# The mean of the first tile by an add-and-accumulate over two half rows, in place of a sum over 512 elements, with the first turns reordered

## The chip, the cores and the metric

One core of a Trainium2 chip. The metric is the device time of one execution in microseconds (us); several executions were taken of each kernel and their median is quoted. A ratio is the mean time of one kernel's runs over that of the other's runs of the same rounds, so it is not quite the ratio of the medians that stand beside it. Faster or slower needs 2%. Where the text calls a kernel slower, it means only that its 95% interval lies clear of 1.

## The reference, cut to what matters

```python
x = A_x                                  # (1, 2048, 512) bf16: 16 tiles of 128 rows
xn = _layernorm(x, axis=-1)
return x + _A_ref(xn, ...) + _B_ref(xn, B_w_gate, B_w_up, B_w_down)
# _B_ref: (gelu(xn @ w_gate) * (xn @ w_up)) @ w_down, 512 -> 1376 -> 512
```

The first matrix work that can start is `xn @ w_gate` and `xn @ w_up` for the first tiles. The kernel does not wait for the whole normalisation there: it multiplies the *centred* rows, x minus mean, and brings in the division by the standard deviation when it reads the result.

## The kernel before

The parts that the change touches. `V`, `ACT` and `PE` record an operation on VectorE (DVE), ScalarE (ACT) and TensorE (PE) with an estimated duration. A list scheduler orders what was recorded: PE and the queue of loads on SyncE stay in program order, DVE, ACT and GpSimd are ordered by the estimates, and `ch` chains some DVE operations in a fixed order. A filler is a small matmul whose result nobody reads, put in to give PE something to do (0.31 us each in the profile before). A transpose of `cent_T` is a matmul on PE, too (0.22 us at full pace), and ACT then copies its result out (0.28 us for 128 columns), so that PE can use it as weights.

```python
ch(V(lambda e: e.tensor_reduce(SUM0.ap, X[0].ap, mybir.AxisListType.X, ALU.add), 600, [X[0]], [SUM0], "sum0"))
ch(cent(0, 0), cent(0, 1))        # tile 0: D*x - sum, columns 0..127 and 128..511
fill(2)                           # two filler matmuls on PE
cent_T(0, 0, 1, 7)                # PE transpose of the first 128 columns, ACT copies it out (times 1/D)
ch(cent(1, 0), cent(1, 1))        # tile 1: x + (-mean), its mean comes from ACT
fill(1)
ev0 = cent_T(0, 1, 4, 5, True)    # the other three transposes of tile 0
ev1 = cent_T(1, 0, 1, 6)          # the first transpose of tile 1
S.order_behind(ev0(), ev1)        # ACT copies tile 1's first one out ahead of tile 0's other three
ks(0, 0, [0], True)               # k=0, tile 0, gate half: two matmuls of 256 columns
ks(0, 0, [1])                     # the same with the up half
cent_T(1, 1, 4, 7)
ks(0, 1, [0], True)
ks(0, 1, [1])                     # k=0, tile 1
# ... statistics of tile 2 on DVE ...
ks(1, 0, [0])
ks(1, 0, [1])                     # k=1, tile 0: needs the up slice of k=1
cent_T(2, 0, 1, 6)                # transposes of tile 2, and so on
```

The weights of the first 512 columns are loaded in slices of 128 KB, gate and up in turn for k = 0, 1, 2, 3, behind tile 0 of x in one queue. Tiles 1 and 2 of x go through ACT's queue.

## Time and profile before

| | before |
|---|---|
| median of 3 runs before the prediction | 177.34 us (177.23 to 177.38) |
| span in the profile | 175.5 us |
| PE busy | 171.9 us, 98% |
| PE alone, without a hole, from | 6.23 us to 173.56 us |

The span is the time inside the program; the run adds some 1.3 us around it (the profiled run took 176.79 us). PE's busy time is no proof that it is at its best (the warm-up's matmuls of 512 columns follow one another at 0.42 us, later ones at 0.22, and both count as busy), but a chain that is PE alone from 6.23 us to the end says that only what happens before 6.23 us, or a hole made later, can move the time. The lines for this are in the prediction below.

### The profile page before, as it was taken

To read this page: it belongs to the slowest core of one execution; us is meant where nothing else is said; L and a number is where in the kernel's file an instruction comes from. 1 tells how busy PE (TensorE), PEld (TensorE's weight loads), DVE (VectorE), ACT (ScalarE), POOL (GpSimd) and SP (SyncE) were. 2 spreads that over 40 slices of the span, in tenths; PEclk is the share of its full clock that TensorE was granted. 3 is DMA by queue.
4 is the path that set the end of the run, shared out by engine and by line. 5 is a ranking of instruction groups with operands and counts; after the bars stand their busy time and mean duration, and the time that the engine had idled before them with its cause. 6 is when DMAs were issued, how large, how long until landed. Compare 5 with 4: busy or idle time off the path is not lost.

```text
span 175.5 us, 2504 instructions
## 1 busy us (share of the span) xinstructions
PE 171.9 (98%) x876; PEld 84.9 (48%) x891; DVE 160.1 (91%) x278; ACT 95.2 (54%) x187; POOL 10.8 (6%) x24
## 2 busy tenths in 40 slices
PE   8999999999999999999999999999999999999995
PEld 3546464845544444444644444444464444444453
DVE  6987999997989999799999999999999999999931
ACT  5474768999767898465676792000657960000000
POOL 3222030203000000002000000000000000000000
DMA  5999999985998000002033000002001000000311
GB/s 170 242 334 141 268 145 218 114 130 112 195 289 231 4 0 2 0 30 78 15 73 78 0 0 0 4 0 90 30 0 30 4 0 0 0 0 0 120 65 60
DMA packets 32420, 14.36 MB, mean 82 GB/s; under 512 B 23736, under 2 KB 32408, under 8 KB 32408
## 3 DMA queue, kind: packets, MB, share of 16 engines
q1 hardware_dynamic: 32096, 13.94, 34.7%
q10 hardware_dynamic: 312, 0.27, 0.5%
q8 instruction: 7, 0.11, 0.3%
q14 instruction: 5, 0.04, 0.1%
HBM read 6.46 MB, written 2.10 MB: 49 GB/s over the span
## 4 chain that ended last, share of the span: by engine, by line
PE 95%; DMA 2%; SPq 1%; issue 1%; DVE 0%
PE PS L885 37%; PE PS L844 32%; PE PS L750 16%; PE PS L713 4%; PE PS L818 3%; PE PS L702 2%; DMA arena<-in_B_w_up_dram 2%; SPq L484 1%; PE PS L680 0%; SPq L493 0%; DVE arena L903 0%
## 5 line engine op out<-in xcount | busy, mean ns | idle before, releaser
L885 PE MATMUL PS<-arena 128*128 128x512 bf16 (+3 forms) x317 | 65.9, 366 | 0.3
L844 PE MATMUL PS<-arena 128*128 128x512 bf16 x257 | 57.1, 379 | 0.4
L885 PEld LDWEIGHTS PS<-arena 128*128 128x128 bf16 (+1 forms) x323 | 30.8, 98 | 35.2
L844 PEld LDWEIGHTS PS<-arena 128*128 128x128 bf16 x264 | 25.8, 98 | 30.2
L788 DVE TENSOR_TENSOR_SCAN arena<-arena 128x512 bf16<-128x512 f32 x32 | 38.8, 1254 | 0.0
L859 ACT ACTIVATE arena<-PS 128x512 bf16<-128x512 f32 x33 | 19.7, 598 | 25.1 <-DVE arena L903 16.7
L750 PE MATMUL PS<-arena 128*128 128x512 bf16 (+1 forms) x142 | 28.1, 355 | 0.1
L863 ACT ACTIVATE arena<-PS 128x512 bf16<-128x512 f32 x33 | 19.8, 599 | 5.0 <-PE PS L844 4.9
L750 PEld LDWEIGHTS PS<-arena 128*128 128x128 bf16 x144 | 14.1, 98 | 13.3
L877 ACT ACTIVATE PS<-arena 128x512 f32<-128x512 bf16 (+2 forms) x17 | 9.6, 581 | 19.7 <-DVE arena L903 19.0
L759 ACT ACTIVATE arena<-PS 128x512 bf16<-128x512 f32 x32 | 17.5, 596 | 1.5 <-PE PS L750 1.5
L903 DVE TENSOR_TENSOR arena<-PS,arena 128x512 bf16<-128x512 f32 (+2 forms) x17 | 10.8, 652 | 6.3 <-PE PS L885 6.2
L865 DVE TENSOR_TENSOR arena<-arena 128x512 bf16<-128x512 bf16 x33 | 13.2, 420 | 2.6 <-ACT arena L863 2.4
L800 DVE TENSOR_TENSOR arena<-arena 128x4096 bf16<-128x4096 bf16 x4 | 9.2, 2290 | 0.1
L777 DVE TENSOR_TENSOR arena<-arena 128x4096 bf16<-128x4096 bf16 (+1 forms) x5 | 9.2, 1859 | 0.0
L775 DVE TENSOR_TENSOR arena<-arena 128x4096 bf16<-128x4096 bf16 (+1 forms) x5 | 9.2, 1857 | 0.0
L801 DVE TENSOR_TENSOR arena<-arena 128x4096 bf16<-128x4096 bf16 x4 | 9.1, 2286 | 0.0
L611 DVE BATCH_NORM_STATS2 arena<-arena 128x6 f32<-128x512 bf16 x12 | 7.7, 680 | 0.1
L722 ACT ACTIVATE arena<-PS,arena 128x256 bf16<-128x256 f32 (+1 forms) x16 | 6.1, 447 | 2.3 <-DVE arena L557 1.4
L713 PE MATMUL PS<-arena 128*128 128x512 bf16 (+1 forms) x40 | 7.1, 336 | 0.0
L725 DVE SCALAR_TENSOR_TENSOR arena<-PS,arena 128x256 bf16<-128x256 f32 (+1 forms) x16 | 6.3, 445 | 0.7 <-PE PS L702 0.7
L702 PE MATMUL PS<-arena 128*128 128x512 bf16 (+1 forms) x30 | 6.0, 337 | 0.1
(95 smaller groups left out, 124.7 us busy)
## 6 DMA issues: line engine op xcount, KB each, us to landing
out_dram<-arena SPq DMA_DIRECT2D x15, 128.0 KB, 1.7
arena<-in_A_x_dram SPq DMA_DIRECT2D x3, 512.0 KB, 5.5
arena<-in_B_w_down_dram SPq DMA_DIRECT2D x1, 1280.0 KB, 7.2
arena<-in_B_w_gate_dram SPq DMA_DIRECT2D x4, 128.0 KB, 3.1
arena<-in_B_w_up_dram SPq DMA_DIRECT2D x4, 128.0 KB, 3.5
arena<-in_B_w_gate_dram SPq DMA_DIRECT2D x1, 480.0 KB, 6.7
arena<-in_B_w_up_dram SPq DMA_DIRECT2D x1, 480.0 KB, 7.6
arena<-arena SPq DMA_TRANSPOSE x25, 3.1
```

Of the source, the lines that this page charges most:

```text
L702: PE(lambda e: e.matmul(dst, XCd(j, k), WGU[:, ws[0]:ws[-1] + 1, k, f0:f1], start=first, stop=k == KD - 1, skip_group_check=True), d_pe([w ...
L713: ins_ = e.matmul(dst, XCd(j, k), WGU[:, :, k, f0:f1], start=(k == 0), stop=(k == KD - 1))
L750: ins_ = e.matmul(PS[bank][:, 128 * j0:128 * j1], BBT[c][dk].ap[:, 128 * s:128 * (s + 1)], XNT[b].ap[:, dk, 128 * j0:128 * j1], start=(dk ...
L759: GATE["evBu"] = ACT(lambda e, bank=bank, k3=k3, s=s, c=c: e.activation(SSc[k3][s][c].ap, PS[bank][:, :], ACTF.Copy), d_act(512), [BANK[ba ...
L788: V(lambda e, g=g, rb=rb, init=init: e.tensor_tensor_scan(g.ap, rb, g.ap, init, ALU.mult, ALU.add), d_dve_scan(512), [g, PA[RRr]] + ([CARc ...
L844: ins_ = e.matmul(PS[bank][0:m, c0:c1], W.ap[:, dk, 128 * ft:128 * ft + m], XNT[b].ap[:, dk, c0:c1], start=(dk == 0), stop=(dk == KD - 1))
L859: GATE["last_gelu"] = ACT(lambda e, bg=bg, kk=kk, m=m: e.activation(GG[kk].ap[0:m, :], PS[bg][0:m, :], ACTF.Gelu_apprx_tanh), d_act(512), ...
L863: ACT(lambda e, bu=bu, kk=kk, m=m: e.activation(UPB[kk].ap[0:m, :], PS[bu][0:m, :], ACTF.Copy), d_act(512), [BANK[bu]], [UPB[kk]], "evU")
L865: V(lambda e, kk=kk, m=m, ft=ft, k2=k2: e.tensor_tensor(HTt[k2][ft].ap[0:m, :], GG[kk].ap[0:m, :], UPB[kk].ap[0:m, :], ALU.mult), d_dve_tt ...
L877: ACT(lambda e: e.activation(PS[bank][:, c0:c1], X[tt].ap[:, c0:c1], ACTF.Copy), d_act(c1 - c0), [X[tt]], [BANK[bank]], "seed")
L885: ins_ = e.matmul(PS[bank][:, c0:c1], l_[:, 128 * j:128 * (j + 1)], r_[:, c0:c1], start=False, stop=last and n == len(ops) - 1, skip_group ...
L903: V(lambda e: e.tensor_tensor(OUTB[ko].ap[:, c0:c1], PS[bank][:, c0:c1], XD[tt].ap[:, c0:c1], ALU.add), d_dve_1x(c1 - c0), [BANK[bank], XD ...
```

## The change

Its intent is to have the mean of tile 0 sooner: `tensor_reduce` goes over 512 elements (0.69 us in the profile before), while an addition of the two halves of a row with an accumulator output goes over 256 and gives minus the mean at once. Two filler matmuls go, ACT copies the transposes out in the order in which PE makes them, and tile 1's first transpose moves behind the first two matmuls.

```diff
-            if j == 0:
-                f = lambda e: e.tensor_scalar(XN[j].ap[:, c0:c1], X[j].ap[:, c0:c1], float(D), SUM0.ap, ALU.mult, ALU.subtract)
-            else:
-                f = lambda e: e.tensor_scalar(XN[j].ap[:, c0:c1], X[j].ap[:, c0:c1], NM1.ap, None, ALU.add)
+            nm = NM1 if j else NM0
+            f = lambda e: e.tensor_scalar(XN[j].ap[:, c0:c1], X[j].ap[:, c0:c1], nm.ap, None, ALU.add)
 ...
-        ch(V(lambda e: e.tensor_reduce(SUM0.ap, X[0].ap, mybir.AxisListType.X, ALU.add), 600, [X[0]], [SUM0], "sum0"))
+        hd = D // 2
+        ch(V(lambda e: e.tensor_tensor_reduce(H0[2].ap[:, 0:hd], X[0].ap[:, 0:hd], X[0].ap[:, hd:D], scale=-1.0 / D, scalar=0.0,
+                                              op0=ALU.add, op1=ALU.add, accum_out=NM0.ap), 400, [X[0]], [H0[2], NM0], "mean0"))
         ch(cent(0, 0), cent(0, 1))
-        fill(2)
         cent_T(0, 0, 1, 7)
         ch(cent(1, 0), cent(1, 1))
         fill(1)
-        ev0 = cent_T(0, 1, 4, 5, True)
-        ev1 = cent_T(1, 0, 1, 6)
-        S.order_behind(ev0(), ev1)
+        cent_T(0, 1, 4, 5)
 ...
         ks(0, 0, [0], True)
+        cent_T(1, 0, 1, 6)
         ks(0, 0, [1])
```

In `cent_T` the argument `later` and the scale of 1/D for tile 0 are no longer needed.

More of the change, by code (lines that the diff above doesn't have):

```diff
@@ L474, in build @@
         GATE["iotj"] = POOL(lambda e: e.iota(IOTJ.ap, [[1, 512]], base=0, channel_multiplier=0), 600, [], [IOTJ], "iotj")
-        NM1, SUM0 = A.alloc("NM1", [1], F32), A.alloc("SUM0", [1], F32)
+        NM0, NM1 = (A.alloc(n, [1], F32) for n in ("NM0", "NM1"))
         def ld_x(b):
@@ L672, in build, with cent_T @@
         XNp = [[Buf("XN%d_%d" % (j, n), "sb", XN[j].lo + 256 * n, XN[j].lo + (1024 if n else 256)) for n in range(2)] for j in range(2)]
-        def cent_T(j, k0, k1, bank, later=False):
+        def cent_T(j, k0, k1, bank):
             pt = PS[bank].bitcast(BF16)[:, 0:128 * (k1 - k0)]
@@ L684, in cent_T @@
             w = XCs[j] if k1 - k0 == KD else [XCs[j][k0 > 0]]
-            sc = 1.0 if j else 1.0 / D
-            def evac():
-                GATE["evTA"] = ACT(lambda e: e.activation(dst, src, ACTF.Copy, scale=sc), d_act(128 * (k1 - k0)), [BANK[bank]], w, "evT")
-                return GATE["evTA"]
-            return evac if later else evac()
+            GATE["evTA"] = ACT(lambda e: e.activation(dst, src, ACTF.Copy), d_act(128 * (k1 - k0)), [BANK[bank]], w, "evT")
         FR = ((0, 256), (256, 512), (512, 768), (768, 896))
@@ L960, in cent @@
             c0, c1 = (0, 128) if n == 0 else (128, D)
-            if j == 0:
-                f = lambda e: e.tensor_scalar(XN[j].ap[:, c0:c1], X[j].ap[:, c0:c1], float(D), SUM0.ap, ALU.mult, ALU.subtract)
-            else:
-                f = lambda e: e.tensor_scalar(XN[j].ap[:, c0:c1], X[j].ap[:, c0:c1], NM1.ap, None, ALU.add)
-            return V(f, 100 + 0.5 * (c1 - c0), [X[j], NM1 if j else SUM0], [XNp[j][n]], "sub")
-        ch(V(lambda e: e.tensor_reduce(SUM0.ap, X[0].ap, mybir.AxisListType.X, ALU.add), 600, [X[0]], [SUM0], "sum0"))
+            nm = NM1 if j else NM0
+            f = lambda e: e.tensor_scalar(XN[j].ap[:, c0:c1], X[j].ap[:, c0:c1], nm.ap, None, ALU.add)
+            return V(f, 100 + 0.5 * (c1 - c0), [X[j], nm], [XNp[j][n]], "sub")
+        hd = D // 2
+        ch(V(lambda e: e.tensor_tensor_reduce(H0[2].ap[:, 0:hd], X[0].ap[:, 0:hd], X[0].ap[:, hd:D], scale=-1.0 / D, scalar=0.0,
+                                              op0=ALU.add, op1=ALU.add, accum_out=NM0.ap), 400, [X[0]], [H0[2], NM0], "mean0"))
         ch(cent(0, 0), cent(0, 1))
-        fill(2)
         cent_T(0, 0, 1, 7)
```

## The prediction

> **What bounds the kernel now.** I read the page first, for the engines' shares, then the chain that ended last in order of time, then the timeline of the first 7 us engine by engine, and last the DMA issues in narrow stretches, to get the landing of each load.
>
> The page's head and its chain:
>
> ```profile
> PE 171.9 (98%) x876; PEld 84.9 (48%) x891; DVE 160.1 (91%) x278; ACT 95.2 (54%) x187; POOL 10.8 (6%) x24
> ...
> PE 95%; DMA 2%; SPq 1%; issue 1%; DVE 0%
> ```
>
> TensorE (PE) is busy 98% of a span of 175.5 us, and 95% of the chain is PE. A VectorE (DVE) instruction can only shorten this if PE waits for it somewhere. The only DVE piece in the chain (0%) is the last addition of the output. The chain in order of time shows where PE's unbroken run begins:
>
> ```profile
> 2.60 3.59 DMA arena<-in_B_w_up_dram
> 6.19 0.05 issue
> 6.23 0.39 PE PS L702 x2
> 6.62 0.22 PE PS L680 x4
> 6.85 2.81 PE PS L702 x13
> ```
>
> From 6.23 us to 173.56 us the chain holds nothing but PE and gaps of 0.05 us. It is released at 6.23 by a load: the k=1 slice of the up weights, issued at 2.60 and landed 3.59 us later, at 6.19. The start-up before it is a row of small dependent steps, of which the sum of tile 0 is one:
>
> ```profile
> 2.96 0.69 DVE L967 TENSOR_REDUCE arena<-arena 128x1 f32<-128x512 bf16 x1 [0.63 <-DMA arena<-in_A_x_dram]
> 3.68 0.48 DVE L962 TENSOR_SCALAR arena<-arena 128x128 bf16<-128x128 bf16 x2
> 4.13 0.48 DVE L964 TENSOR_SCALAR arena<-arena 128x128 bf16<-128x128 bf16 x2
> 4.76 0.69 DVE L611 BATCH_NORM_STATS2 arena<-arena 128x6 f32<-128x512 bf16 x1
> ...
> 3.83 0.19 ACT L956 ACTIVATION_READ_ACCUMULATOR arena<-arena 128x1 f32 x1
> ...
> 6.23 0.11 PEld L702 LDWEIGHTS PS<-arena 128*128 128x128 bf16 x2 [0.33 <-DMA arena<-in_B_w_up_dram]
> ```
>
> The columns are start, duration, what ran, and in brackets the idle time before it and what ended that. Tile 0 arrives at 2.95, the sum ends at 3.65, the two subtractions of tile 0 run from 3.68, its first transpose on PE starts at 4.00. The last line decides: before the matmul of the up weights, k=1, the weight load (PEld) stood idle 0.33 us for a DMA, though everything from DVE and ScalarE (ACT) was there. So PE already had slack in front of this load.
>
> The landings, from the DMA issues asked for in narrow stretches (issue time plus time to landing, rounded to 0.1): tile 1 of x 0.99 + 2.3 = 3.3; gate k=0 1.20 + 2.4 = 3.6; tile 2 of x about 1.43 + 3.3 = 4.7; up k=0 1.66 + 3.3 = 5.0; gate k=1 2.13 + 3.0 = 5.1; up k=1 2.60 + 3.6 = 6.2.
>
> [...]the accumulator read at 3.83 takes 0.19 us behind an activation of 0.63. [...]the seven warm-up matmuls of 512 columns load weights 0.42 us apart, while 49 later ones take 10.74 us, 0.219 us each. [...]the trace has 2.2 us for the first tile and 3.6 for the up slice.[...]
>
> **The change part by part.** It removes the sum (0.69 us) and adds one add-and-accumulate over two halves of 256. [...]With an accumulator read of 0.06 (the step between dependent DVE rows here is some 0.03 to 0.07) to 0.19 us (ACT's row) it comes to 0.48 to 0.61 us; I take 0.5. The mean is then ready at about 3.46 in place of 3.65, a gain of 0.1 to 0.2 us. The rate could be higher, since a tensor_tensor of 128x512 bf16 takes only 0.42 us in this trace, but the accumulation makes me doubt it.
>
> Tile 0's subtractions use the mean itself in place of D*x minus the sum: same shapes, same 0.48 us for both. They end at about 3.97 rather than 4.16. Tile 1's subtractions wait for ACT's mean, which ends at 3.83 + 0.19 = 4.02, so they move only from 4.13 to about 4.08. The statistics of tile 2 at 4.76 wait for the tile itself (landing about 4.7), and do not move; nor does anything of DVE behind them.
>
> On PE the two filler matmuls before the first transpose go, one stays; the first transpose moves from 4.00 to about 3.8, its evacuation on ACT from 4.32 to about 4.05, and the first real matmul (gate, k=0) from 4.74 to about 4.45. The second pair (up, k=0) needs a load that landed at about 5.0; it starts at 4.96 in the trace, the moment the load is there, and stays. Then the transposes of tile 1, the pair of gate k=0 and the pair of up k=0 for tile 1, and gate k=1 for tile 0 follow in the same set as before, and all this must be done by 6.19, when up k=1 lands. Moved earlier by 0.2 us or not at all, PE waits there. From 6.23 on the program order on PE is that of before. So the sum on the path is **0.0 us**: gain 0.15 to 0.2 at the start, all of it turned into a longer wait for up k=0 and up k=1.
>
> The last part is the order on ACT. Before, the evacuation of tile 1's first transpose (0.28 us) was forced ahead of tile 0's other three (0.49). Now it comes behind. Worked out: tile 0's first 4.05 to 4.33, its other three 4.35 to 4.84, tile 1's first 4.86 to 5.14 (before: 4.87 to 5.15, equal within the guess), tile 1's other three 5.3 to 5.8. PE then has tile 1's four k=0 matmuls from about 5.3 and the gate k=1 pair by 5.7 to 5.9, six matmuls of 0.11 us: in time for 6.19, with 0.3 us to spare. Cost 0.
>
> **The rivals.** (a) The gain goes straight through to the end: 177.34 - 0.2 = 177.15. For it speaks that the sum stands on the path to the first matmul. Against it stand the two landings at 5.0 and 6.2, and the 0.33 us of idle. (b) [...]Against it: the warm-up ends only at 3.92 and the first transpose now follows at 3.8, so there is hardly a hole. (c) The new operation is slower than I think; the trace has no row of it. It may take up to 0.69 + 0.3 = 1.0 us before PE feels it; at 1.5 us it would cost about 0.5, 177.8. (d) The order of later DVE and ACT work is chosen by the kernel's list scheduler from estimated durations; the estimate here falls from 600 to 400 ns and orders far downstream may flip. With PE full, a flip can hardly gain, but could open a hole of some tenths: 177.3 to 178.
>
> **Range and chances.** The centre is the time before, 177.3: cause and slack both say zero. The three runs before lie within 0.15 us of each other. Down I allow 0.4 for an earlier landing of the up slice or part of (a); up I allow 0.6 for (c), (d) and a little of (b). So 176.9 to 177.9. A change of 2% is 3.5 us; nothing named gains that, and only (b) and (d) together approach a loss of it: faster 0.01, same 0.97, slower 0.02.
>
> **What would show each step right or wrong.** In the profile of the changed kernel the new DVE operation starts at about 2.96 and gives way to the subtraction at about 3.46 (right if within 3.35 to 3.6). The first transpose starts near 3.8, the first matmul with gate weights near 4.45, the one with up weights still at about 4.96. The weight load that waits for the up slice is still released at 6.2, with at least as long an idle before it as 0.33, and the chain from there is PE alone for 167.3 us. The statistics of tile 2 stay at 4.76. I am wrong if the release at 6.2 is by ACT or DVE and not by a DMA, if the load lands at another time because loads moved, if PE's rows keep half pace behind 4.3, or if PE shows holes later that were not there.

Rival (b) came to about +1.4 us, 178.8: it was my guess that without the two fillers PE would keep its half pace longer.

"Clock" and "the release of the clock", in the expectations below, are words for what the rows show of PE's pace: in the profile after three transposes take 0.32 us of the chain at half pace (at 4.13) and 0.17 at full pace (at 5.48). The granted clock is 1.0 in every run, and 1.00 in the profile after both from 0.8 to 4.4 us and from 5.2 to 8.0, so what lies behind the two paces is not shown.

## The result, and the profile after

| | before | after |
|---|---|---|
| median | 177.31 us (176.98 to 177.39, 6 runs) | 177.12 us (176.77 to 177.23, 6 runs) |
| ratio | | 0.9987, 95% interval 0.9974 to 1.0000 |
| span in the profile | 175.5 us | 175.5 us |

The medians differ by 0.19 us, which is just what the rival of a gain that passes through had forecast (177.15). So one comparison does not separate "nothing" from "all of it", and the experiments had to.

The head of the page and the chain's shares, after:

```profile
PE 172.7 (98%) x889; PEld 84.9 (48%) x889; DVE 159.6 (91%) x279; ACT 95.9 (55%) x187; POOL 10.7 (6%) x24
...
PE 98%; DVE 0%; issue 0%
```

PE has 889 matmul records here and 876 before, though this program has two fewer of them: some were missing from the trace before, so the 0.8 us more of PE is no finding. What is new is that no load stands in the chain any more. The same chain in order of time (start, duration, what):

```profile
0.77 3.15 PE PS L929 x7
3.92 0.11 PE PS L680
4.03 0.11 PE PS L936
4.13 0.32 PE PS L680 x3
...
4.48 0.59 PE PS L697 x2
5.07 0.11 PE PS L680
5.18 0.30 PE PS L697 x2
5.48 0.17 PE PS L680 x3
5.65 0.95 PE PS L697 x8
6.59 0.22 PE PS L680 x4
```

L929 is the warm-up, L680 the transposes, L697 the matmuls of the first turns. In this execution PE is in the chain from the warm-up on. The transposes of tile 2 (the last line; 6.62 before) come 0.03 us earlier than before, and the matmuls of the second stage start at 10.92 rather than 10.96. So the profiled execution shows a gain of 0.04 us at the end of the first turns, where the mean itself came 0.25 us earlier. Its timeline (start, duration, engine, operation, and in brackets the idle time before it and what ended that):

```profile
2.92 0.43 DVE L961 CUSTOM_DVE_ANT_0 arena<-arena 128x256 bf16<-128x256 bf16 x1 [0.59 <-DMA arena<-in_A_x_dram]
3.27 0.08 DVE L961 DVE_READ_ACCUMULATOR2_ANT arena<- 128x1 f32 x1
3.39 0.48 DVE L957 TENSOR_SCALAR arena<-arena 128x128 bf16<-128x128 bf16 x2
3.70 0.10 PEld L680 LDWEIGHTS PS<-arena 128*128 128x128 bf16 x1 [0.69 <-DVE arena L957]
4.09 0.48 DVE L957 TENSOR_SCALAR arena<-arena 128x128 bf16<-128x128 bf16 x2 [0.22 <-ACT arena L951]
4.48 0.59 PE L697 MATMUL PS<-arena 128*128 128x256 bf16 x2
4.97 0.51 PE L697 MATMUL PS<-arena 128*128 128x256 bf16 x2
5.21 0.28 ACT L685 ACTIVATE arena<-PS 128x128 bf16<-128x128 bf16 x1 [0.23 <-PE PS L680]
5.55 1.05 PE L697 MATMUL PS<-arena 128*128 128x256 bf16 x8
```

The new operation takes 0.43 us and its accumulator read, which overlaps its end, is done at 3.35. The subtractions of tile 0 follow at 3.39, which is 0.47 us after the start of the operation; before it was 0.72. So the mean is 0.25 us sooner. But tile 1's subtractions still wait for ACT, at 4.09 (4.13 before), and the pair with the up half of k=0 starts at 4.97 (4.96 before). The pair of matmuls at 4.48 takes 0.59 us in two overlapping rows; the first two such rows before took 0.38. PE is still at half pace here: a transpose takes 0.31 us and a matmul of 256 columns 0.42, against 0.22 and 0.27 from the three transposes at 5.32 on. Before, the turn came between 4.52 and 4.74 (two rows of PE):

```profile
4.52 0.31 PE L680 MATMUL PS<-arena 128*128 128x128 bf16 x1
4.74 0.27 PE L702 MATMUL PS<-arena 128*128 128x256 bf16 x1
```

This is where the gain went in this execution. The first matmul is 0.26 us earlier (4.48 for 4.74), but the gate pair needs 0.38 us up to the next matmul (4.48 to 4.86) where it needed 0.22 (4.74 to 4.96), and tile 1's transpose, 0.11, now stands before the up pair: 0.38 + 0.11 - 0.22 = 0.27. The up slice of k=0, landed at 1.66 + 3.2 = 4.9, holds nothing up here.

### The profile page after: what moved, and what is told of

Its sections match the earlier page's. It is cut to its first block, busy times and chain, and to the rows that moved or that the text cites. A ratio compares the mean times of both kernels' runs of the same rounds, so it can differ in the third digit from the quotient of the medians.

```text
span 175.5 us, 2521 instructions
## 1 busy us (share of the span) xinstructions
PE 172.7 (98%) x889; PEld 84.9 (48%) x889; DVE 159.6 (91%) x279; ACT 95.9 (55%) x187; POOL 10.7 (6%) x24
## 4 chain that ended last, share of the span: by engine, by line
PE 98%; DVE 0%; issue 0%
PE PS L880 37%; PE PS L839 32%; PE PS L745 16%; PE PS L708 4%; PE PS L697 3%; PE PS L813 3%; PE PS L929 2%; PE PS L680 1%; DVE arena L898 0%; PE PS L936 0%
## 5 line engine op out<-in xcount | busy, mean ns | idle before, releaser
L839 PE MATMUL PS<-arena 128*128 128x512 bf16 x264 | 58.1, 379 | 0.0
L720 DVE SCALAR_TENSOR_TENSOR arena<-PS,arena 128x256 bf16<-128x256 f32 (+1 forms) x16 | 6.3, 443 | 0.4 <-PE PS L697 0.4
L697 PE MATMUL PS<-arena 128*128 128x512 bf16 (+1 forms) x30 | 6.3, 350 | 0.0
```

The costliest lines, as they stand in the source:

```text
L697: PE(lambda e: e.matmul(dst, XCd(j, k), WGU[:, ws[0]:ws[-1] + 1, k, f0:f1], start=first, stop=k == KD - 1, skip_group_check=True), d_pe([w ...
L839: ins_ = e.matmul(PS[bank][0:m, c0:c1], W.ap[:, dk, 128 * ft:128 * ft + m], XNT[b].ap[:, dk, c0:c1], start=(dk == 0), stop=(dk == KD - 1))
```

## The experiments

All twelve runs were in three groups of four; each group ran on one chip with its own runs of before, six executions of each kernel and eleven of before. The differences looked for are a few tenths of a us, and the executions of one kernel in one group spread over 0.5 to 1.1 us, three far ones at 179 us left aside, so I lean on the profiles' rows where the times cannot decide.

One reading serves all of them. Call *start* the moment at which the 40 matmuls of the second stage (6.93 us in the chain, where there is no hole) begin: 10.96 before, 10.92 after. The span minus this start is 164.5 to 164.6 us in the nine profiles (before, after, a_after, b_op_only, c_order_only, d_after_fill, g_load_late, n_after_again, q_none_pinned) where PE has no hole behind it and the turns of the two kernels are kept: 175.5 - 10.96 = 164.5 before, 175.5 - 10.92 = 164.6 after. So the whole difference between such executions arises before 12 us.

### Group one: the parts one by one

**a_after.** The changed kernel, unedited, timed once more.

> The changed kernel itself, once more and timed closely. Load theory (the landing of the up weights of k=1 near 6.0 to 6.2 us sets the start of PE's unbroken run, the earlier mean ends in a longer wait): 177.2 to 177.4, ratio to before within 0.9985 to 1.0005. Pass-through theory (the earlier mean goes to the end): 0.2 us faster, ratio 0.9988 or less with an interval clear of 1. Clock theory[...]: warm pace again only from about 5.2 us in the profile, where before has it from 4.2.

Measured: 177.03 us, before 176.91, ratio 1.0008 (0.9986 to 1.0031). The gain of 0.19 us is not repeated. The chain of this profile:

```profile
1.66 3.60 DMA arena<-in_B_w_up_dram
5.25 0.05 issue
5.30 0.39 PE PS L697 x2
5.69 0.17 PE PS L680 x3
5.86 0.87 PE PS L697 x8
...
11.06 6.93 PE PS L708 x40
```

Here the chain does begin with a load, but with the up slice of k=0 (issued 1.66, landed 5.26), not with that of k=1. And PE is at full pace from the first transpose on (0.23 us at 3.73), with one filler. The clock theory, my guess that with fewer fillers PE turns to full pace some 1 us later, had asked for half pace until 5.2 us. It fails. (That before has full pace from 4.2 is a misreading in the expectation; its transpose at 4.52 is still at half pace, as shown above.)

**b_op_only.** Before, with the new operation alone.

```diff
-ch(V(lambda e: e.tensor_reduce(SUM0.ap, X[0].ap, mybir.AxisListType.X, ALU.add), 600, [X[0]], [SUM0], "sum0"))
+ch(V(lambda e: e.tensor_tensor_reduce(H0[2].ap[:, 0:hd], X[0].ap[:, 0:hd], X[0].ap[:, hd:D], scale=1.0, scalar=0.0,
+                                      op0=ALU.add, op1=ALU.add, accum_out=SUM0.ap), 400, [X[0]], [H0[2], SUM0], "sum0"))
```

> Before with the add-and-accumulate alone (same fillers, same order of turns and evacuations). Mean ready near 3.38 in place of 3.65. Load theory: time of before within 0.1 us, the wait of the weight load for the up slice grows from 0.33 to about 0.4 to 0.6. Pass-through theory: 0.2 us faster. Clock theory: full pace from 4.2 as in before.

Measured: 176.79 us, before 176.91, ratio 0.9989 (0.9970 to 1.0008). It is the lowest median of this group, but the interval holds both nothing and 0.2 us. In this execution the up slices landed early (k=0 at 1.66 + 3.0 = 4.7, k=1 at 2.60 + 3.2 = 5.8), PE waited for neither, so the longer wait that was expected is a miss, and the start was 10.66. PE was at full pace from about 4.4 (0.28 us for the two transposes at 4.35). The first transpose came at 3.93, because the fillers held PE until then: its subtractions had begun at 3.31 already. In c_order_only, without those fillers and with the old sum, it came at 4.04; only both parts of the change together bring it to 3.71.

**c_order_only.** The changed order, with the sum over 512 elements kept (tile 0 as D*x minus the sum, and the scale of 1/D when it is copied out, as before).

```diff
-ch(V(lambda e: e.tensor_tensor_reduce(..., accum_out=NM0.ap), 400, [X[0]], [H0[2], NM0], "mean0"))
+ch(V(lambda e: e.tensor_reduce(SUM0.ap, X[0].ap, mybir.AxisListType.X, ALU.add), 600, [X[0]], [SUM0], "sum0"))
```

> The changed order and fewer fillers, with the sum over 512 elements kept. Load theory: time of before within 0.1 us. If the gain of the changed kernel is one of the order, it is here too (0.1 to 0.2 us faster). Clock theory: as in the changed kernel the pace is half until about 5.2 us, and with the mean 0.27 us later the first turns end 0.1 to 0.3 us later than before: 177.4 to 177.6.

Measured: 177.19 us (one execution at 179.15), ratio 1.0028 (0.9986 to 1.0069). In the profile PE's weight loads wait for both up slices, 0.27 us for k=0 at 5.28 and 0.33 us for k=1 (landed 6.5) at 6.54, the start is 11.27, and the pace turns at about 4.8 us with one filler (0.31 us for the transpose at 4.46, 0.27 for the matmul at 4.91). The chain of this profile runs through the sum (3.01, 0.69 us) and has only 0.05 us of waiting before each of the two matmuls: here the sum and the loads end nearly together.

**d_after_fill.** The changed kernel with `fill(2)` put back ahead of the first transpose.

> The changed kernel with the two filler matmuls of before put back ahead of the first transpose. Clock theory: full pace from about 4.2 us again, first turns end 0.1 to 0.2 us earlier than in the changed kernel, up to the landing of the up slice: 176.9 to 177.1. Load theory without a role for the clock: no difference to the changed kernel beyond 0.1 us. If the release of the clock is a matter of chance from run to run and not of the fillers, the pace changes somewhere between 4 and 5.5 us here as well.

Measured: 177.35 us, ratio 1.0014 (0.9995 to 1.0033): no faster. The transpose at 5.08 us is still at half pace (0.31 us), with the fillers. Across the fourteen profiles the pace turns between 3.7 us (a_after) and 6.7 us (n_after_again) with one filler, and between 4.4 us (b_op_only) and 6.3 us (r_gate_first) with three. The two ranges overlap and one and the same program has both early and late turns, so the fillers do not decide it; what does, these runs do not show.

This run makes a pair with a_after: the same order, PE at full pace behind the load in both. Here the load let PE go at 5.70 and the start was 11.46; there 5.30 and 11.06. Both are 5.76 us apart. The load landed 0.40 us later here (5.65 against 5.26), and everything behind it moved by 0.40 us.

### Group two: the mean later, the mean away, the loads moved

**f_mean_twice.** The add-and-accumulate done twice, the first into a place that nobody reads.

```diff
+ch(V(lambda e: e.tensor_tensor_reduce(..., accum_out=NMX.ap), 400, [X[0]], [H0[2], NMX], "mean0x"))
 ch(V(lambda e: e.tensor_tensor_reduce(..., accum_out=NM0.ap), 400, [X[0]], [H0[2], NM0], "mean0"))
```

> The changed kernel with the add-and-accumulate done twice, the first into a place that nobody reads: the mean comes about 0.46 us later, at 3.85 in place of 3.39. Load theory (landings of the up slices set the start of PE's unbroken run): the first transpose goes from 3.7 to about 4.15, the first matmul with gate weights to about 4.9, and the up slices still decide, since they land at 4.7 to 5.6 and 5.8 to 6.5: 0 to 0.2 us slower than the changed kernel. Pass-through theory: 0.46 us slower, 177.5 where before is at 177.

Measured: 177.67 us, before 176.99, ratio 1.0032 (1.0011 to 1.0053). On the time alone the pass-through theory wins. The profile says otherwise. The subtractions of tile 0 are at 3.81, and the transposes of tile 2 at 6.54, where a_after has 6.57: the later mean is gone by then. The loss sits 10 us further on; its chain:

```profile
7.81 7.46 DMA arena<-arena
...
15.40 1.03 POOL arena L553
...
16.53 0.06 DVE arena L554
...
17.03 0.49 DVE arena L720
...
17.66 1.46 PE PS L708 x8
```

L554 is the first DVE operation on the parameters of the other branch. It waits for GpSimd, and that for a transposing load (a DMA_TRANSPOSE row, 7.46 us from issue to landing) that landed at 15.27. The added operation changed the estimates, the scheduler moved L554 ahead of four of the products (L720) that read PE's results (PE goes on at 17.66, behind the one of 17.03 + 0.49): six stand before it in this program's order of DVE, ten in the changed kernel's. DVE stood at it for 2.8 us (0.9 in both a_after and the first profile of the changed kernel). Worked out from the start that the transposes imply (6.54 + 4.49 = 11.03, 4.49 being 11.06 - 6.57 in a_after), the span would be 11.03 + 164.6 = 175.6; it is 176.6. The hole cost 1.0 us, and the later mean nothing that shows.

**i_no_mean.** The mean of tile 0 taken away; zero is added in its place. (`cent` takes `nm.ap if j else 0.0`, and the operation is gone.) Wrong in tile 0, by its small mean.

> The changed kernel without the mean of tile 0: zero is added to tile 0 in its place, so the result is wrong on purpose in tile 0 by its small mean (it may still pass the tolerance). Subtractions of tile 0 start at 2.95 in place of 3.39. Load theory: no faster than the changed kernel, within 0.1 us. Pass-through theory: 0.44 us faster than it. A third cause, the warm-up matmuls that hold PE until about 3.7 and the mean of tile 1 that holds ScalarE until 4.0, says the same as the load theory in time, and would show in the profile as a first transpose at 3.7 all the same.

Measured: 177.41 us, ratio 1.0028 (1.0009 to 1.0047): slower, without the operation. The first transpose is at 3.71, as with it. The load for up k=0 is waited for at 5.12. The start is 10.98, but behind it PE has a hole of some 0.2 us (175.8 - 10.98 - 164.6) at 16.2 us: the chain goes through a 0.49 us product on DVE there, and L554 waits 2.1 us, because the order flipped here too (seven products stand before it). So this time is no measure of the mean either, and both runs had to be repeated with the order held.

**g_load_late.** One more load of 128 KB in the queue ahead of the up slice of k=0.

```diff
 ld_wk(WG, WGc, ins["B_w_gate"], k)
+if k == 0:
+    S.dma(lambda e: e.dma_start(WD.ap[:, 0, :], ins["B_w_down"][0:128, :]), 128 * 1024, writes=[WDc[0]], tag="extra")
 ld_wk(WU, WUc, ins["B_w_up"], k)
```

> The changed kernel with one more load of 128 KB put into the queue ahead of the up slice of k=0, so that it and everything behind it is issued about 0.45 us later. Load theory: both up slices land 0.3 to 0.6 us later and the unbroken run starts as much later: 177.3 to 177.7 where before is at 177. Pass-through theory: nothing, because the mean and the first transposes are where they were.

Measured: 177.39 us, ratio 1.0050 (1.0007 to 1.0094), with two of the six executions at 179.2 and 179.4, for which I have no profile. The interval is clear of 1 only by these two: the other four have a mean of 177.26, which is 1.0011 of the mean of before. And the profile does not carry the load theory's delay: the up slice of k=0, issued 0.47 us later, landed at 5.2, no later than in other executions (4.7 to 5.65); that of k=1 landed at about 6.4 (5.8 to 6.5 elsewhere). PE's weight loads waited for both (0.40 and 0.21 us). The start was 11.12. The extra traffic is no clean delay; the run is inconclusive for the size.

**k_hold.** The loads from the gate slice of k=2 on held back until the gate slice of k=0 has landed.

```diff
-ld_wk(WG, WGc, ins["B_w_gate"], k)
+GATE["wg%d" % k] = ld_wk(WG, WGc, ins["B_w_gate"], k, [GATE["wg0"]] if k == 2 else ())
```

> The changed kernel with the gate slice of k=2, and so all loads behind it in that queue, held back until the gate slice of k=0 has landed (issue at about 3.65 in place of 3.07), to take traffic away from the up slices of k=0 and k=1. Load theory: the up slice of k=1 lands 0.1 to 0.4 us earlier and the run starts as much earlier: 176.7 to 176.9 where before is at 177, if no later load is now waited for. Pass-through theory: nothing. If the landing time hangs on latency and not on shared traffic: no earlier landing and no gain.

Measured: 177.25 us, ratio 1.0010 (0.9991 to 1.0029): no gain. The later loads were issued at 3.58 in place of 3.07. The up slice of k=0 landed at 5.24, no earlier; that of k=1 at 2.60 + 3.2 = 5.8, but it was no longer what PE waited for. And behind the start (11.13) the weight load now stood 0.9 us, and PE itself 0.63, near 18.6 us for transposing loads of the normalised tiles, which are later in the same queue.

### Group three: the order held

**n_after_again.** The changed kernel a third time, as the yardstick of the group.

> The changed kernel a third time, as the yardstick for the two pinned runs of this job. Both theories: the same as before within 0.2 us; no hole in PE between 11 and 20 us.

Measured: 177.26 us, before 177.29, ratio 1.0011 (0.9990 to 1.0033). No hole. Its chain, to be laid beside that of a_after, which is the same program:

```profile
1.66 3.65 DMA arena<-in_B_w_up_dram
5.31 0.05 issue
5.36 0.61 PE PS L697 x2
5.97 0.32 PE PS L680 x3
6.29 1.15 PE PS L697 x8
...
11.77 6.93 PE PS L708 x40
```

The load let PE go at 5.36, against 5.30 there. The same 13 steps took 2.08 us (0.61 + 0.32 + 1.15) against 1.43, because PE kept half pace until about 6.7 us. The start is 0.71 us later, of which 0.06 is the load and 0.65 the pace. The spans are 176.3 and 175.7. The turn of the pace and the landings, which differ from one execution to the next, move one and the same program by more than the 0.25 us by which the mean came sooner.

**p_twice_pinned.** The add-and-accumulate twice, but given to the scheduler as one operation with the estimate of one, so that every engine's order is that of the changed kernel.

```diff
+def mean0(e):
+    e.tensor_tensor_reduce(H0[1].ap[:, 0:hd], X[0].ap[:, 0:hd], X[0].ap[:, hd:D], ..., accum_out=NMX.ap)
+    return e.tensor_tensor_reduce(H0[2].ap[:, 0:hd], X[0].ap[:, 0:hd], X[0].ap[:, hd:D], ..., accum_out=NM0.ap)
+ch(V(mean0, 400, [X[0]], [H0[1], H0[2], NM0, NMX], "mean0"))
```

> The changed kernel with the add-and-accumulate twice, given to the scheduler as one operation of the same estimate, so that every engine's order is that of the changed kernel. Mean 0.46 us later. Load theory: 0 to 0.2 us slower than the changed kernel, first transpose about 4.1 us, the up slices still decide, no hole of PE near 16 us (the hole of the unpinned run came from a flip in VectorE's order ahead of a wait for the parameters). Pass-through theory: 0.46 us slower than the changed kernel. If the loss of the unpinned run (0.6 us) came from the later mean and not from the flip, it is here too.

Measured: 177.55 us, ratio 1.0013 (0.9987 to 1.0040), against 1.0011 of the changed kernel in the same group. The first transpose and the load that lets PE go, in PE's weight loads:

```profile
3.98 0.10 PEld L680 LDWEIGHTS PS<-arena 128*128 128x128 bf16 x1 [0.96 <-DVE arena L957]
...
5.63 0.11 PEld L697 LDWEIGHTS PS<-arena 128*128 128x128 bf16 x2 [0.59 <-DMA arena<-in_B_w_up_dram]
```

The subtractions began at 3.67 (3.34 in n_after_again), the first transpose at 3.98 (3.71), and then the weight load still stands idle for 0.59 us for the up slice. That is not PE's own idle time: the weight load before it, at 4.89, ran 0.21 us ahead of its matmul at 5.10. PE itself has a hole of 0.22 us:

```profile
5.10 0.31 PE L680 MATMUL PS<-arena 128*128 128x128 bf16 x1
5.64 0.39 PE L697 MATMUL PS<-arena 128*128 128x256 bf16 x2 [0.22 <-DMA arena<-in_B_w_up_dram]
```

From the matmuls that it let go (5.64) to the start (11.40) it is 5.76 us, exactly as in a_after and d_after_fill. The later mean has vanished in the wait for the load. The slice landed 0.28 us later here than in n_after_again, but that is not what hides the mean: behind the transpose at 5.10 the pair could have started at 5.21 (0.11 later, as 4.97 follows 4.86 in the first profile of the changed kernel), and in n_after_again it did not start before 5.36. Of the hole near 16 us there is nothing, so that came from the flip. The expectation "no hole" held only there: near 18.7 the weight load stood 0.7 us, and PE itself 0.46, for a transposing load, as in k_hold. Its landing (4.40 us after issue) is part of that; what else delays it, I leave open.

**q_none_pinned.** A store of zero in place of the mean, again the same operation in the scheduler's eyes. Wrong in tile 0.

```diff
-ch(V(lambda e: e.tensor_tensor_reduce(..., accum_out=NM0.ap), 400, [X[0]], [H0[2], NM0], "mean0"))
+ch(V(lambda e: e.memset(NM0.ap, 0.0), 400, [X[0]], [H0[2], NM0], "mean0"))
```

> The changed kernel with a store of zero in place of the mean (wrong on purpose in tile 0 by its small mean), same operation in the scheduler's eyes, so that every engine's order is that of the changed kernel. Subtraction of tile 0 some 0.4 us earlier. Load theory: same as the changed kernel within 0.1 us. Pass-through theory: 0.4 us faster. No hole of PE near 16 us.

Measured: 177.25 us, ratio 1.0002 (0.9979 to 1.0024). The same two places in its profile, with the matmul of the first transpose between them:

```profile
3.34 0.10 PEld L680 LDWEIGHTS PS<-arena 128*128 128x128 bf16 x1 [0.33 <-DVE arena L957]
...
3.71 0.31 PE L680 MATMUL PS<-arena 128*128 128x128 bf16 x1
...
5.38 0.13 PEld L697 LDWEIGHTS PS<-arena 128*128 128x128 bf16 x2 [0.58 <-DMA arena<-in_B_w_up_dram]
```

The weights of the first transpose are ready 0.30 us sooner than in n_after_again (3.64), but its matmul starts at 3.71 all the same: the last warm-up matmul, begun at 3.29, holds PE until then. The weight load's wait for the up slice is 0.58 us, where n_after_again has 0.56. Without the whole operation nothing was gained that a run could show. But the gain ended at the warm-up here and never reached the load, so this run says where an earlier mean stops, and only p_twice_pinned says what the load hides.

**r_gate_first.** b_op_only with the gate halves of both tiles ahead of the up halves of both.

```diff
 ks(0, 0, [0], True)
-ks(0, 0, [1])
 cent_T(1, 1, 4, 7)
 ks(0, 1, [0], True)
+ks(0, 0, [1])
 ks(0, 1, [1])
 ...
 ks(1, 0, [0])
+ks(1, 1, [0])
 ks(1, 0, [1])
+ks(1, 1, [1])
 cent_T(2, 0, 1, 6)
 cent_T(2, 1, 4, 7)
-ks(1, 1, [0, 1])
```

> Before with the add-and-accumulate and with the first turns ordered by the landings: the gate halves of both tiles ahead of the up halves of both, for k=0 and k=1, and the third tile's transposes behind them. PE then has 0.2 to 0.4 us of work to do while it waits for the up slices. Load theory: 0.1 to 0.3 us faster than before, 176.7 to 176.9 where before is at 177, unless the later order of VectorE opens a hole near 16 us. If the waits for the up slices do not set the end: no difference.

Measured: 177.67 us, before 177.29, ratio 1.0028 (1.0008 to 1.0049): a miss. PE no longer waited for an up slice, but it no longer had work while ACT copied tile 2's transposes out: at 7.96 us it stood 0.20 us for that copy. And in the profiled execution PE was at half pace until about 6.3 us. The start was 11.81. How much of the loss of 0.4 us is the order and how much that chance, one profile does not say. No version of these beat before clearly.

## Why the prediction was right or wrong, point by point

**The time and the range: right.** 177.3 was predicted, 177.12 measured. Three comparisons of the two kernels, each on its own rounds, give 0.9987, 1.0008 and 1.0011, on both sides of 1 and within 0.25 us of it.

**The new operation: right in kind, a little small in gain.** The main part takes 0.43 us (0.42 to 0.43 in every profile that has it). The doubt about a higher rate was right: 256 columns take as long as the 512 of the plain tensor_tensor (0.42 us). The accumulator read is a row of its own, but takes 0.08 us and lies inside the end of the main row. So the sum of 0.48 to 0.61 was too large: 0.43 from start to mean, and a gain of 0.25 where 0.1 to 0.2 was said.

**The rows of the start: right, one by luck.** The first transpose came at 3.71 for about 3.8, the first matmul at 4.48 for about 4.45, tile 1's subtractions at 4.09 for about 4.08. The statistics of tile 2 came at 4.64 for 4.76, with their tile, which landed 0.1 us earlier. The up half of k=0 at 4.97 for about 4.96 is luck: it was to start when its load lands, but in that execution the load was there and half pace and the moved transpose gave the same number.

**The gain turns into a wait for a load: right in part.** With the mean 0.33 us later (p_twice_pinned) the weight load still stands 0.59 us for the up slice, and the start follows that landing. But the load is not the only place where a gain ends. With the operation away (q_none_pinned) it ends at the warm-up, which holds PE until 3.71, and in the first profile of the changed kernel and in b_op_only no load holds PE at all and the chain is PE from the warm-up on. The prediction did not name this second place. The times alone would not show any of this: their intervals are some 0.4 us wide to each side.

**The slack of 0.33 us: too large.** That is the idle of the weight load. The matmul before, at 5.91, is followed at full pace by one at 6.02, and the held one started at 6.23: PE itself lost 0.21 us.

**"The weight load that waits for the up slice is still released at 6.2": wrong.** This is the step that failed: in the first profile of the changed kernel no load holds PE, and in those of a_after and n_after_again it is the slice of k=0 (5.30 and 5.36) and not of k=1. I took one execution's landings as fixed. Between the two slices PE has two matmuls, three transposes and six matmuls, 8 x 0.109 + 3 x 0.056 = 1.04 us at full pace (in a_after 0.87 us for eight matmuls, 0.17 for three transposes). Before, the slices landed 1.2 us apart (5.0 and 6.2), so the second one held PE; in a_after 0.7 us apart (5.3 and 6.0), so the first one did. Which one it is depends on the execution, and the outcome does not. The first tile landed 2.2 us after its issue, before and after; the up slice of k=0, of the same size and third in the queue, took from 3.0 us (b_op_only) to 4.0 (d_after_fill).

**The order on ACT: right only at full pace.** Tile 1's first transpose was to be copied out at 4.86, equal to before. It was at 4.89 in a_after, at full pace, but at 5.21 in the first profile, since PE makes that transpose only behind the first pair of matmuls, which took half pace there. That took the 0.3 us to spare which I had counted there.

**The half pace (rival b): there, but not by the fillers.** I argued that hardly a hole would arise and took 4.2 for the turn to full pace. That was misread: before itself keeps half pace in its transpose at 4.52, behind the 4.3 that I had named as a sign of being wrong. The turn came at about 5.2 in the profile of the result, then at 3.7 and 6.7 in two more of the same program, and with three fillers at about 4.7, 4.4 and 6.3 in before, b_op_only and r_gate_first. PE's first matmul was at 0.77 us in the first two of these, so the turn came 4.4 and 2.9 us behind it. A late turn costs less than the 1.4 us that I gave it: 0.65 between a_after and n_after_again.

**The scheduler's flips (rival d): right as a danger, and not met by this change.** Its own profiles have no hole in PE. Two of the experiments did meet it, with a hole of 1.0 us in f_mean_twice.

## What to carry to other kernels

Before you shorten an operation, look for what the engine behind it does and waits for next: if a load or work of its own stands there, the gain can end in a longer wait (here the up slice, still waited for 0.59 us in p_twice_pinned, or the warm-up, which held PE to 3.71 in q_none_pinned), and taking the operation out altogether is a cheap test, if you then read in the rows where the gain stopped. Where a scheduler orders by estimates, an experiment that adds or removes an operation can flip an order far downstream (the 1.0 us of f_mean_twice, at 16 us); hold the order, or read in the profile where the difference sits before believing the time. When the effect sought is smaller than the spread of the executions, compare rows of profiles (the landing, and the distance from it to the next stage) and not medians.
